# The last two chunks' sums shared with GpSimd, the last chunk's norm on ScalarE, and a new order table

## The chip, the cores and the metric

One core of a Trainium2 chip. The time is the device time of one execution, in microseconds, given as the median of several executions. All the executions quoted count as fast ones in the record. Profiles are of one execution each; its span is about 1.8 us shorter than its time.

## The reference, cut to what matters

```python
x = A_x
x = x + _A_ref(_layernorm(x), ...)   # a state-space layer with complex states
x = x + _B_ref(_layernorm(x), ...)   # a long convolution by FFT, times q (here: the normalised x)
x = x + _A_ref(_layernorm(x), ...)
x = x + _B_ref(_layernorm(x), ...)
return x                             # (1, 2048, 640)
```

The convolution result of B, called Y below, does not depend on x and is made once, in the first part of the kernel. Applying B is then only `x + layernorm(x) * Y`. The kernel works in four chunks of 512 rows, each of four tiles of 128 x 640.

## The kernel before: the parts that matter

Every piece of work is a task with an engine and a priority. A small scheduler runs when the program is built, not on the chip: it simulates the engines with estimated durations and takes the ready task with the lowest number in a table WHEN. The result is one fixed order of instructions for each engine.

```python
WHEN = {"kv_lk0": 0, ..., "a_t0": 26.17, ..., "yt_nsi": 30.27, ..., "yq0_VA:m0": 31.92, ...}   # 862 entries, cut

def run(self):                      # cut
    ...
    when = WHEN[t.name]
    t.rank, t.wait = (-when[0], when[1]) if isinstance(when, tuple) else (-when, 0.3)
    ...
    t = max(cands, key=lambda t: (t.rank, -t.idx))     # among the tasks ready for this engine
    ...
    order.sort(key=lambda t: (t.start, t.idx))         # start as the scheduler's simulation has it
    for t in order:
        t.emit(t.eng)
```

Two tasks that will matter fill tables that are needed much later. Beside them stand the copies out of PSUM, which free the accumulator buffers for TensorE (in the changed kernel TensorE waits 2.77 us for one such copy):

```python
def e_t0(_):                                           # task a_t0, VectorE; read by task a_t1 on ScalarE
    v.tensor_scalar(r, y, MAGIC, None, ALU.add)        # 128 x 1290, f32
    v.scalar_tensor_tensor(r, r, MAGIC, y, ALU.subtract, ALU.subtract)

def e_nsi(_):                                          # task yt_nsi, VectorE: the sign of one table
    nc.vector.tensor_scalar(T["NSi"].get(), T["Si"].get(), -1.0, None, ALU.mult)

def evac(nc, eng, out, in_):                           # a copy out of PSUM
    if eng == "act":
        nc.scalar.activation(out, in_, ACT.Copy)
    else:
        nc.vector.tensor_copy(out, in_)
```

The end of the kernel, B applied to the last chunk tile by tile (the groups have one tile each):

```python
if len(qs) == 1:
    ... nc.vector.scalar_tensor_tensor(b, x, nmean, Y, ALU.add, ALU.mult)     # (x - mean) * Y
    ... nc.vector.scalar_tensor_tensor(Y, b, rstd, x, ALU.mult, ALU.add)      # * rstd + x
else:
    ... ln_apply(...)                                                         # ScalarE or VectorE
    ... nc.vector.tensor_tensor(b, b, Y, ALU.mult)
    ... nc.vector.tensor_tensor(Y, b, x, ALU.add)
```

## Time and profile before

| | before |
|---|---|
| time, median of 3 first runs | 358.5 us (357.69 to 358.55) |
| span of the profiled execution | 356.8 us |
| TensorE busy | 327.5 us, 92% |
| VectorE busy | 315.1 us, 88% |
| ScalarE busy | 256.4 us, 72% |
| last residual sum begins (the last matmul is done) | 345.89 us |

The last row is the best divider of this kernel: what comes before it is ruled by TensorE (327.5 of 345.9 us busy), what comes after it is an 11 us tail of VectorE, ScalarE and one store. The lines themselves stand in the prediction.

### The profile page before, as it was taken

Reading aid. Unit: us, or ns where it says so; the run is one execution under the profiler, and the core shown is the slowest. Engines: PE = TensorE matmul, PEld = TensorE weight load, DVE = VectorE, ACT = ScalarE, POOL = GpSimd, SP = SyncE. Lnnn points to the kernel's source line nnn. Section 1 sums busy time; section 2 is a strip of 40 time slices with the busy share of each in tenths; the row PEclk is TensorE's granted clock in tenths of the full one; section 3 lists DMA queues with packets and bytes.
Section 4 is the critical chain, followed back from the end, with each engine's and each line's share of the span. In section 5 each row is a group of like instructions: output and inputs, shape, how many; then the busy total and the mean of one; then the engine's idle time right before and its main releaser. Section 6 shows DMA issues by size and latency. Waiting matters only on the chain.

```text
span 356.8 us, 8409 instructions
## 1 busy us (share of the span) xinstructions
PE 327.5 (92%) x3534; PEld 247.6 (69%) x3565; DVE 315.1 (88%) x479; ACT 256.4 (72%) x406; POOL 20.8 (6%) x51
## 2 busy tenths in 40 slices
PE   7686998989998997999999999999999999999970
PEld 7346876867686986986685677686866767755640
DVE  8799798798799797999999969979999679999896
ACT  3999798898799999943378599797256577306850
POOL 5841003000000000000000000000000000000000
PEclk9999899999999999999999999999999999999996
DMA  7999999999999982790226690605032022220141
GB/s 193 208 235 188 182 184 217 193 186 202 237 245 163 184 174 46 144 233 2 62 73 119 137 333 34 147 18 132 0 68 81 3 16 59 75 75 2 50 172 73
DMA packets 118712, 45.91 MB, mean 129 GB/s; under 512 B 111629, under 2 KB 112914, under 8 KB 118674
## 3 DMA queue, kind: packets, MB, share of 16 engines
q1 hardware_dynamic: 118528, 45.36, 59.9%
q8 instruction: 28, 0.46, 0.5%
q14 instruction: 10, 0.08, 0.1%
q10 hardware_dynamic: 146, 0.01, 0.0%
HBM read 17.38 MB, written 7.86 MB: 71 GB/s over the span
## 4 chain that ended last, share of the span: by engine, by line
PE 69%; ACT 10%; DVE 8%; DMA 7%; issue 3%; SPq 2%; DVEq 0%; ACTq 0%
PE ps L859 31%; PE ps L770 11%; PE ps L773 11%; ACT b L382 6%; PE ps L608 3%; PE ps L1163 3%; DMA b<-in_A_C_im_dram 2%; DMA b<-in_B_v_dram 2%; DVE b L1169 2%; PE ps L1313 2%; DMA b<-b 2%; PE ps L1314 1%; PE ps L1208 1%; SPq L536 1%; DMA b<-in_B_k_dram 1%
## 5 line engine op out<-in xcount | busy, mean ns | idle before, releaser
L382 ACT ACTIVATE b<-ps 128x1024 bf16<-128x1024 f32 (+3 forms) x125 | 109.6, 945 | 29.5 <-PE ps L773 25.5
L859 PEld LDWEIGHTS <-b 128*128 128x128 bf16 x880 | 67.7, 98 | 48.3
L859 PE MATMUL ps<-W,b 128*128 128x128 bf16 (+1 forms) x629 | 95.7, 298 | 0.6
L770 PE MATMUL ps<-b,BT 128*128 128x256 bf16 x400 | 56.8, 273 | 0.0
L773 PE MATMUL ps<-b,BT 128*128 128x256 bf16 x400 | 56.7, 273 | 0.0
L808 DVE TENSOR_TENSOR_SCAN b<-rtab,b 128x1290 bf16<-128x1290 f32 x16 | 44.7, 2833 | 0.3
L773 PEld LDWEIGHTS <-BT 128*128 128x128 bf16 x400 | 39.1, 98 | 4.5
L770 PEld LDWEIGHTS <-BT 128*128 128x128 bf16 x400 | 38.6, 98 | 4.4
L726 ACT ACTIVATE b<-b,nmr,rstd 128x640 bf16<-128x640 f32 (+1 forms) x43 | 37.0, 915 | 6.2 <-DVE nmr L693 6.2
L681 ACT ACTIVATE junk<-b,nmean 128x640 bf16<-128x640 f32 x48 | 39.7, 828 | 1.5
L1232 PE MATMUL ps<-b,b 128*128 128x128 bf16 x170 | 35.1, 219 | 1.2 <-ACT G L382 0.7
L1235 PE MATMUL ps<-b,b 128*128 128x128 bf16 x170 | 35.4, 219 | 0.0
L1237 PE MATMUL ps<-b,b 128*128 128x128 bf16 x150 | 32.8, 219 | 0.0
L1234 PE MATMUL ps<-b,b 128*128 128x128 bf16 x150 | 32.8, 219 | 0.0
L384 DVE CAST b<-ps 128x1024 bf16<-128x1024 f32 (+2 forms) x24 | 26.2, 1109 | 6.3 <-PE ps L1208 2.7
L867 ACT ACTIVATE b<-ps 128x640 f32<-128x640 f32 x16 | 11.1, 697 | 22.8 <-PE ps L859 22.8
L859 PE MATMUL ps<-G,b 128*128 128x128 bf16 (+1 forms) x152 | 26.5, 295 | 0.4
L1163 PE MATMUL ps<-b,fd 128*128 128x512 bf16 x73 | 18.6, 380 | 3.8 <-POOL fd L1141 2.0
L1313 PE MATMUL ps<-b,b 128*128 128x128 bf16 x160 | 19.4, 219 | 2.6 <-ACT b L382 2.1
L1314 PE MATMUL ps<-b,b 128*128 128x128 bf16 x160 | 19.2, 219 | 0.0
L552 ACT ACTIVATE b<-b,s_F 128x640 f32<-128x640 bf16 x20 | 17.2, 859 | 1.8 <-DVE W L556 1.4
L556 DVE SCALAR_TENSOR_TENSOR W<-b,s_F 128x640 bf16<-128x640 bf16 x20 | 17.4, 882 | 1.0 <-ACT b L552 0.7
(210 smaller groups left out, 560.3 us busy)
## 6 DMA issues: line engine op xcount, KB each, us to landing
b<-in_A_x_dram SPq DMA_DIRECT2D x8, 640.0 KB, 4.9
b<-ysd SPq DMA_DIRECT2D x8, 640.0 KB, 5.1
b<-in_B_ssm_k_dram SPq DMA_DIRECT2D x5, 512.0 KB, 8.6
kvd<-b SPq DMA_DIRECT2D x5, 512.0 KB, 4.3
b<-kvd SPq DMA_DIRECT2D x5, 512.0 KB, 5.4
ysd<-b SPq DMA_DIRECT2D x5, 512.0 KB, 5.0
out_dram<-b SPq DMA_DIRECT2D x8, 320.0 KB, 2.2
tab<-in_A_B_re_dram SPq DMA_DIRECT2D x1, 800.0 KB, 7.4
```

The lines of the kernel that those rows point to most:

```text
L382: nc.scalar.activation(out, in_, ACT.Copy)
L681: nc.scalar.activation(small.junk, src(q), ACT.Square, bias=st["nmean"][:, i:i + 1], scale=1.0, accum_out=st["ssq"][:, i:i + 1])
L726: nc.scalar.activation(dst, src, ACT.Identity, bias=st["nmr"][:, i:i + 1], scale=st["rstd"][:, i:i + 1])
L770: nc.tensor.matmul(pb[:, jj, c2, :], lhsT=aw["BT1"][:, c2, j, k, :], rhs=uT[:, 0:2, k, :], start=(k == 0), stop=False)
L773: nc.tensor.matmul(pb[:, jj, c2, :], lhsT=aw["BT0"][:, c2, k, j * P:(j + 1) * P], rhs=uT[:, 2:4, k, :], start=False, stop=(k == NJ - 1))
L808: nc.vector.tensor_tensor_scan(gv, rt, gv, 0.0, ALU.mult, ALU.add)
L859: nc.tensor.matmul(pc[:, o0:o1], lhsT=lh, rhs=rh, start=(n == 0), stop=(n == len(ops) - 1))
L1163: nc.tensor.matmul(pk[:, 512 * b:512 * (b + 1)], lhsT=s_ds.get()[:, l, :], rhs=kT[:, t0:t0 + 512], start=(l == 0), stop=(l == 3))
L1232: nc.tensor.matmul(ps[:, g, 0, :], lhsT=T["Cf"].get()[:, q, :], rhs=are, start=True, stop=single)
L1234: nc.tensor.matmul(ps[:, g, 0, :], lhsT=T["Sf"].get()[:, q, :], rhs=A[:, 2 * q + 1, :], start=False, stop=True)
L1235: nc.tensor.matmul(ps[:, g, 1, :], lhsT=T["NSf"].get()[:, q, :], rhs=are, start=True, stop=single)
L1237: nc.tensor.matmul(ps[:, g, 1, :], lhsT=T["Cf"].get()[:, q, :], rhs=A[:, 2 * q + 1, :], start=False, stop=True)
```

## The change

Its intent: VectorE is the second busiest engine and alone in the tail. Of the four last tiles, three get their norm from ScalarE, sums may go to GpSimd, which is idle there (20.8 us busy in the whole span, nothing after 60 us), and each tile is stored when it is done. As this changes the tasks, the order table was searched anew.

```diff
 WHEN = {
-    (862 entries)
+    (867 entries: nearly every number is another)
 }
@@ b_chunk
-        if out is not None and q % 2 == 1:
+        if out is None:
+            return
+        if len(groups) > 1:
+            ... one store for each tile of 128 rows
+        elif q % 2 == 1:
             ... one store for two tiles
@@
-            if len(qs) == 1:
+            if qs[0] == 3:
                 ... the pair of two-input instructions
@@
-                        else:
-                            nc.vector.tensor_tensor(s_Y.get()[:, q, :], b, x, ALU.add)
-                    t_m = S.add(f"{nm}_m:{q}", "dve", 0.83 if out is None else 0.77, [t_mm], ...)
+                        else:
+                            (nc.gpsimd if eng == "pool" else nc.vector).tensor_tensor(s_Y.get()[:, q, :], b, x, ALU.add)
+                    engs, ests = (("dve", "pool"), (0.77, 1.4)) if out is not None and c >= NCH - 2 else ("dve", 0.83 if out is None else 0.77)
+                    t_m = S.add(f"{nm}_m:{q}", engs, ests, [t_mm], ...)
```

## The prediction

The sum for the tail came to -0.6 us: -1.8 us for the norm on ScalarE and -0.1 us for the single stores, and about +1.3 us for the lock. "The lock" is the name for the longer times of GpSimd's and VectorE's instructions beside each other; the trace shows them around 25 us (2.67 us below), but not how long they would be in the tail, so the +1.3 us were not shown. Without the lock the sum was -1.9 us. The 0.41 us for the multiply are 0.49 us less 0.08 us of overlap (the pair's instructions of 0.88 us step by 0.80). The 0.49 us can be had from the trace before, as an estimate: the products all in bf16 take 1.29 us for 128x2176 and 1.49 us for 128x2560, and a line through the two gives 0.49 us at 128x640.

> **What bounds the kernel now.** I read the page first (busy shares, then the 40 slices), then busy time by stretches of the span, then the last pieces of the chain of waits and the timeline of the end. Every reading below is of the one profiled execution, 356.8 us long (358.5 us is the median of the timed runs).
>
> ```profile
> PE 327.5 (92%) x3534; PEld 247.6 (69%) x3565; DVE 315.1 (88%) x479; ACT 256.4 (72%) x406; POOL 20.8 (6%) x51
> ...
> POOL 5841003000000000000000000000000000000000
> ```
>
> TensorE is the busiest engine, VectorE is close behind, and GpSimd does nothing after its first setup work. Where is TensorE's missing 8%? The stretches say (columns: busy us and instruction count of PE, PEld, DVE, ACT, POOL, then granted clock, DMA share, GB/s):
>
> ```profile
> 0.00:36.00 36.00, 26.33 (x323) 20.65 (x325) 30.84 (x99) 29.40 (x45) 17.83 (x45) 1.00 0.99 208
> 36.00:72.00 36.00, 33.83 (x511) 27.71 (x509) 29.32 (x30) 32.18 (x39) 2.94 (x6) 0.95 1.05 192
> 72.00:108.00 36.00, 34.47 (x462) 26.16 (x466) 30.96 (x50) 31.37 (x42) 0.00 (x0) 1.00 1.12 216
> 108.00:144.00 36.00, 32.27 (x478) 28.45 (x477) 30.68 (x50) 35.52 (x44) 0.00 (x0) 1.00 0.79 137
> 144.00:180.00 36.00, 35.90 (x371) 28.27 (x372) 34.86 (x32) 18.91 (x27) 0.00 (x0) 1.00 0.52 111
> 180.00:345.80 165.80, 164.75 (x1404) 116.39 (x1419) 150.71 (x211) 107.60 (x208) 0.00 (x0) 1.00 0.31 82
> 345.80:356.80 11.00, 0.00 (x0) 0.00 (x0) 7.69 (x13) 1.42 (x4) 0.00 (x0) 0.73 0.30 119
> ```
>
> Three regimes. The head, 0 to 144 us, leaves TensorE idle 9.7 + 2.2 + 1.5 + 3.7 = 17.1 us. From 144 to 345.8 us it is idle 1.2 us: this is its own work and no reordering shortens it. The tail, 11.0 us after the last matmul, is all idle. So the time is head idle plus TensorE work plus tail; the change can gain only in the head (by the new order table) and in the tail.
>
> The tail, from the timeline:
>
> ```profile
> 345.89 0.81 DVE L871 SCALAR_TENSOR_TENSOR b<-ps,b 128x640 f32<-128x640 f32 x1
> 346.63 0.88 DVE L901 SCALAR_TENSOR_TENSOR b<-b,nmean,b 128x640 bf16<-128x640 f32 x1
> 347.55 0.89 DVE L905 SCALAR_TENSOR_TENSOR b<-b,rstd,b 128x640 bf16<-128x640 bf16 x1
> 348.35 2.47 DVE L901 SCALAR_TENSOR_TENSOR b<-b,nmean,b 128x640 bf16<-128x640 f32 x3
> 350.86 1.68 DVE L905 SCALAR_TENSOR_TENSOR b<-b,rstd,b 128x640 bf16<-128x640 bf16 x2
> 352.45 0.16 DVE L691 RECIPROCAL rstd<-std 128x1 f32<-128x1 f32 x1
> 352.72 0.88 DVE L905 SCALAR_TENSOR_TENSOR b<-b,rstd,b 128x640 bf16<-128x640 bf16 x1
> 353.63 0.33 SPq L887 DMA_DIRECT2D out_dram<-b  x1
> ```
>
> After the last residual sum (L871) VectorE alone works: eight two-input instructions for the four tiles of the last chunk, each starting 0.80 us after the one before, ending at 353.60, then one store; 3.2 us later the program ends. ScalarE is done at 348.2 us.
>
> [...] This trace's GpSimd tensor_tensor of 128x128 takes a median 394 ns[...]. [...]
>
> ```profile
> 25.12 0.33 DVE L481 TENSOR_SCALAR s_lam<-s_lam 128x5 f32<-128x5 f32 x1
> 25.48 2.31 DVE L487 TENSOR_TENSOR b<-ident_bf,s_lam 128x1920 bf16<-128x1920 bf16 x1
> ...
> 25.38 2.67 POOL L1141 TENSOR_TENSOR fd<-ident_bf,skf 128x128 bf16<-128x128 bf16 x2
> ```
>
> Two GpSimd instructions that take 0.39 us each elsewhere take 2.67 us around a 2.31 us VectorE one; and 128x5 instructions beside GpSimd take 0.33 to 0.37 us against 0.16 us. [...] 128x2560 all bf16 takes 1.49 us, yet the sum with a float32 input 0.82 us for a quarter of that.
>
> **The change part by part.** Every engine's instruction order of the changed kernel was read beside the old one. TensorE has 7123 rows in both: no work is added to it.
>
> *Last chunk, norm by ScalarE.* For three of four tiles the pair "add mean, times Y" and "times rstd, plus x" (2 x 0.80 us) becomes a ScalarE normalisation (0.91 us, as L726 in this profile), a bf16 multiply and a sum. [...] the sum steps by 0.74 us (three in 2.29 us). The fourth tile keeps the old pair. Old tail after the last residual sum: 346.63 to 353.60, 6.97 us. New order there on VectorE: multiply, multiply, sum, pair's first half, reciprocal and product, pair's second half, multiply, sum: 0.41 x 2 + 0.74 + 0.80 + 0.27 + 0.80 + 0.41 + 0.82 = 4.66 us, plus about 0.5 us of hand-overs (0.1 us each at dependent steps, as between 347.43 and 347.55): 5.2 us. ScalarE's statistics of the last tile end at 348.23 in the old timing, before VectorE's reciprocal would come (349.1), and its normalisation, 0.91 us, lies beside the pair's second half, 0.80 us. So the tail is 1.8 us shorter, if nothing contends.
>
> *Sums on GpSimd.* Only three move: two of the last but one chunk and one of the last. They take three times 0.74 us off VectorE[...]. [...]
>
> *Single stores.* 160 KB instead of 320 KB last; issue 0.33 us and 2.2 us to landing are mostly not size: -0.1 us, an estimate.
>
> [...]
>
> *The new order table.* It moves nearly every instruction of the head: the small multiplications that feed GpSimd's first tables now stand 7th in TensorE's order instead of second, the other half of the B matrix is loaded first. The 17.1 us of head idle can grow or shrink; the numbers in the table are priorities, and I take no time from them. Nothing in the profile gives a sign. I put 0 with a spread of about 2 us.
>
> Predicted: 358.5 - 0.6 = 357.9, rounded down a little because a tuned kernel is seldom given a new table that was seen to lose: 357.5 us.
>
> **The rivals.** First, no lock at the tail: GpSimd's sums hide and the tail gives its full 1.9 us, 356.6 us. [...] Against it: the 2.67 us above. Second, the lock in full plus a late last residual sum: 358.5 us or slightly more, the change pays nothing; for it speaks that VectorE is busy without a gap from 345.89 on[...]. Third, the head decides: TensorE waits for a transfer or a table that now comes later, 360 us or 355 us; for it speaks that the DMA share is about 1.0 in the first 108 us[...], and that the first 36 us alone hold 9.7 us of idle.
>
> **Range and chances.** Tail -1.9 to +0.4, head -2.5 to +2.5 in eight of ten: 355.0 to 360.5 us. Two per cent is 7.2 us, more than the whole gain open to the tail and over 40% of the head's idle: faster 0.02, slower 0.03, same 0.95.
>
> **What would show it.** In the changed profile: from the last residual sum's end to VectorE's last end, 5.2 us means no lock[...]. The last ScalarE normalisation must lie beside the pair's second half. TensorE's idle up to 144 us, 17.1 us before, gives the table's part; if it moves by over 3 us the head decided and the tail's story is secondary. The stretch from 144 us to the last matmul must hold about 1 us of idle again; if it holds several, the new order starved TensorE late and my division of the time is wrong.

## The result

The changed kernel takes 363.04 us (median of 4 runs, 362.35 to 363.43), the kernel before 358.38 us in the same rounds. The ratio is 1.0132, 95% interval 1.0111 to 1.0153. All ratios here are the mean time of one kernel's fast runs over that of the other's of the same rounds, so they are not quite the ratio of the medians quoted. Within 2% that is "the same"; in fact the kernel is slower, clear of the noise, and the time lies outside the predicted range.

**Where it went.** The last residual sum begins at 351.43 us instead of 345.89: 5.54 us are lost before it. After it the tail is 361.4 - 351.43 = 10.0 us instead of 10.9: about 1 us is won there. So the tail did what it was meant to do and the rest of the program was made slower. The same stretches of the span as in the prediction, for the changed kernel (the same columns; the last stretch begins just before the last residual sum):

```profile
0.00:36.00 36.00, 29.62 (x327) 22.57 (x327) 31.31 (x98) 27.10 (x44) 17.86 (x45) 0.91 0.97 198
36.00:72.00 36.00, 32.15 (x446) 25.81 (x445) 28.63 (x29) 27.91 (x36) 2.25 (x6) 0.91 0.96 175
72.00:108.00 36.00, 32.97 (x465) 24.88 (x460) 27.55 (x33) 30.79 (x38) 0.00 (x0) 1.00 1.05 217
108.00:144.00 36.00, 33.09 (x482) 28.79 (x480) 32.15 (x64) 35.85 (x48) 0.00 (x0) 1.00 0.81 157
...
351.30:361.40 10.10, 0.10 (x2) 0.00 (x0) 6.69 (x11) 3.24 (x6) 1.59 (x1) 0.72 0.27 97
```

Here lies a trap. TensorE's idle time up to 144 us is 6.4 + 3.9 + 3.0 + 2.9 = 16.2 us, less than the 17.1 us before, and still the head lost over 5 us. Idle time of a fixed stretch says little when the amount of work done in it differs. Look at the counts instead: weight loads up to 144 us (one belongs to each matmul, and no record of them is missing: both traces hold 3565) were 325 + 509 + 466 + 477 = 1777 before and are 327 + 445 + 460 + 480 = 1712 now. All but one of the 65 missing ones are in the second stretch, 445 instead of 509, and there the granted clock is 0.91. At a lower clock TensorE counts as busy for longer with the same work: a matmul of 128x128 takes 0.31 us in this stretch at half clock and 0.22 us before it.

**What happens around 36 us.** VectorE and TensorE of the changed kernel, from the timeline (start, duration, engine, line, operation; in square brackets the idle time before and what ended it):

```profile
35.02 0.83 DVE L639 TENSOR_SCALAR b<-rtab 128x1290 f32<-128x1290 f32 x1
35.88 1.50 DVE L640 SCALAR_TENSOR_TENSOR b<-b,rtab 128x1290 f32<-128x1290 f32 x1
37.30 0.72 DVE L1000 TENSOR_SCALAR b<-b 128x2176 bf16<-128x2176 bf16 x1
37.94 2.35 DVE L385 CAST b<-ps 128x1024 bf16<-128x1024 f32 x2
...
```

```profile
39.21 0.61 PE L1217 MATMUL ps<-FA,b 64*128 64x128 bf16 x8 [2.77 <-DVE b L385]
```

The first two lines are the task a_t0, the third is yt_nsi. They take 37.94 - 35.02 = 2.92 us, and only then come two copies out of PSUM (CAST). TensorE waits 2.77 us for the first of them. From within this wait on, from 38.2 to 45.0 us by the trace's clock record, TensorE has half its clock. The kernel before has the same tasks, but elsewhere:

```profile
28.85 0.82 DVE L638 TENSOR_SCALAR b<-rtab 128x1290 f32<-128x1290 f32 x1
...
34.25 0.72 DVE L991 TENSOR_SCALAR b<-b 128x2176 bf16<-128x2176 bf16 x1
34.88 0.82 DVE L384 CAST BT<-ps 128x640 bf16<-128x640 f32 x1
```

There a_t0 holds nobody up, and only the 0.72 us of yt_nsi stand before a copy that TensorE waits for (1.7 us). Both tables mean a_t0 to come earlier than it does: the old one puts it at 26.17 us and it ran at 28.85, 2.7 us late; the new one puts it at 28.86 and it ran at 35.02, 6.2 us late. (The table holds priorities, but here they can be read as times: the scheduler's own simulation, run again from the two kernels, starts this task at 25.97 and at 28.77 us.) The new table puts the first copy behind it, for tile yq0_VA, at 31.78 us; it ran at 37.94. So in the new order VectorE reaches this place about 6 us behind its plan; the order is fixed, and the urgent copy, behind 2.92 us of the two tasks, came at 37.94 us.

**The tail.** VectorE from the last residual sum on, and GpSimd's sum:

```profile
351.43 0.82 DVE L872 SCALAR_TENSOR_TENSOR b<-ps,b 128x640 f32<-128x640 f32 x1 [0.18 <-PE ps L860]
...
352.18 0.89 DVE L924 TENSOR_TENSOR b<-b,b 128x640 bf16<-128x640 bf16 x2
353.11 1.91 DVE L932 TENSOR_TENSOR b<-b,b 128x640 bf16<-128x640 bf16 x1
...
357.60 0.82 DVE L932 TENSOR_TENSOR b<-b,b 128x640 bf16<-128x640 bf16 x1
```

```profile
347.23 4.01 POOL L932 TENSOR_TENSOR b<-b,b 128x640 bf16<-128x640 bf16 x2 [282.39 <-DVE b L924]
352.75 1.59 POOL L932 TENSOR_TENSOR b<-b,b 128x640 bf16<-128x640 bf16 x1 [1.51 <-DVE b L924]
```

One sum takes VectorE 0.82 us at the end and 1.91 us beside GpSimd's. The residual sum itself waited only 0.18 us, for TensorE: GpSimd did not delay it. From the end of the residual sum (352.18) to VectorE's end (358.42) it is 6.2 us, against 7.0 before.

### The profile page after: what moved, and what is told of

Read it like the earlier page. It is cut to its first block, busy times and chain, and to the rows that moved or that the text cites. A ratio compares the mean times of both kernels' runs of the same rounds, so it can differ in the third digit from the quotient of the medians.

```text
span 361.4 us, 8447 instructions
## 1 busy us (share of the span) xinstructions
PE 334.2 (92%) x3565; PEld 250.6 (69%) x3565; DVE 315.6 (87%) x477; ACT 257.2 (71%) x408; POOL 25.7 (7%) x54
## 4 chain that ended last, share of the span: by engine, by line
PE 57%; ACT 5%; DMA 2%; DVE 1%; issue 1%; ACTq 0%
PE ps L860 33%; PE ps L771 10%; PE ps L774 10%; ACT b L383 2%; DMA b<-b 2%; PE ps L1322 1%; PE ps L1323 1%; DVE b L932 1%; ACT rtab L649 0%; ACT tab L647 0%; PE ps L1241 0%; ACT L645 0%; ACT tab L645 0%; PE ps L1217 0%; ACT rtab L646 0%
## 5 line engine op out<-in xcount | busy, mean ns | idle before, releaser
L383 ACT ACTIVATE b<-ps 128x1024 bf16<-128x1024 f32 (+2 forms) x123 | 106.0, 923 | 36.6 <-PE ps L774 26.2
L1241 PE MATMUL ps<-b,b 128*128 128x128 bf16 x170 | 35.6, 222 | 3.2 <-ACT b L383 2.7
L385 DVE CAST b<-ps 128x1024 bf16<-128x1024 f32 (+1 forms) x26 | 30.3, 1188 | 8.2 <-PE ps L1246 5.2
L1244 PE MATMUL ps<-b,b 128*128 128x128 bf16 x170 | 35.9, 222 | 0.0
L1243 PE MATMUL ps<-b,b 128*128 128x128 bf16 x150 | 33.4, 223 | 0.0
L1246 PE MATMUL ps<-b,b 128*128 128x128 bf16 x150 | 33.4, 222 | 0.0
L860 PE MATMUL ps<-G,b 128*128 128x512 bf16 (+1 forms) x160 | 27.0, 299 | 0.0
L932 POOL TENSOR_TENSOR b<-b,b 128x640 bf16<-128x640 bf16 x3 | 5.6, 1877 | 283.9 <-DVE b L924 283.9
L1172 PE MATMUL ps<-b,fd 128*128 128x512 bf16 x80 | 20.3, 405 | 1.1 <-DVE b L385 0.8
L1322 PE MATMUL ps<-b,b 128*128 128x128 bf16 x160 | 19.2, 219 | 1.7 <-DVE b L1178 1.6
L1217 PE MATMUL ps<-FA,b 64*128 64x128 bf16 x320 | 15.3, 228 | 5.1 <-DVE b L385 2.8
L1323 PE MATMUL ps<-b,b 128*128 128x128 bf16 x160 | 19.1, 219 | 0.0
```

The lines of the kernel that those rows point to most:

```text
L860: nc.tensor.matmul(pc[:, o0:o1], lhsT=lh, rhs=rh, start=(n == 0), stop=(n == len(ops) - 1))
L1241: nc.tensor.matmul(ps[:, g, 0, :], lhsT=T["Cf"].get()[:, q, :], rhs=are, start=True, stop=single)
L1243: nc.tensor.matmul(ps[:, g, 0, :], lhsT=T["Sf"].get()[:, q, :], rhs=A[:, 2 * q + 1, :], start=False, stop=True)
L1244: nc.tensor.matmul(ps[:, g, 1, :], lhsT=T["NSf"].get()[:, q, :], rhs=are, start=True, stop=single)
L1246: nc.tensor.matmul(ps[:, g, 1, :], lhsT=T["Cf"].get()[:, q, :], rhs=A[:, 2 * q + 1, :], start=False, stop=True)
```

## The experiments

Twelve kernels ran, in three groups of four; each is compared with runs of the kernel before on the same chip (medians 358.02, 358.03 and 357.86 us; the third group has the eleven runs of the second and one more). To compare two kernels of different groups, compare their ratios.

### 1 and 2: the table and the tail taken apart

The tasks of the second use of B on its last three chunks and of the last copies of the layer before it make up the tail; all others are the head. In the first kernel the code of the change stays, with the old table's numbers for the head; in the second the old code gets the new table's numbers for the head.

```diff
 # old_table_new_tail: the changed kernel
-WHEN = new table
+WHEN = old table, but the new table's entries for the tail and for the new tasks
 # new_table_old_tail: the kernel before
-WHEN = old table
+WHEN = new table, but the old table's entries for the tail
```

> The changed kernel's code with the old order table for everything but the end (the last chunk's and the two chunks' final multiplications and sums keep the new entries). TensorE's order is that of the kernel before but for the last two groups, which change places. If the loss of 5.5 us up to the last matmul comes from the new table's order of the head, this kernel has its last matmul at 345.8 us as before and the changed tail of 10.0 us: 357.4 us, 1.0 us faster than before. If the loss comes from the code of the tail (GpSimd, stores) in some hidden way, it is near 363 us.

Measured: 356.62 us, ratio 0.9962 (0.9946 to 0.9979). The last residual sum begins at 345.93 us, as before.

> The reverse: the code of before, with the new order table for everything but the end. If the head's order is the cause: last matmul at 351.4 us and the old tail of 11.0 us, 364.0 us. If the tail's code is the cause: 358.4 us.

Measured: 363.12 us, ratio 1.0143 (1.0125 to 1.0161). So the new table costs 1.4% by itself, and the new tail by itself gains 0.4%, some 1.4 us. The prediction's two parts have opposite signs, and the table is the larger one. The split is not perfectly clean: in the second run's trace the last residual sum begins at 349.63 us, only 3.7 us later than before, and what follows it takes 11.7 us instead of 10.9.

### 3: without GpSimd

```diff
-engs, ests = (("dve", "pool"), (0.77, 1.4)) if out is not None and c >= NCH - 2 else ("dve", ...)
+engs, ests = ("dve", ...)
```

> The changed kernel with its three shared sums back on VectorE, nothing else changed. If GpSimd's sums and VectorE's two-input instructions hold each other up[...]: the 1.91 us sum and the 0.81 us small product in the end of VectorE's chain fall back to 0.82 and 0.16 us, and two sums of 0.74 us come back to VectorE before the last residual sum, where there is little room; the tail after the last matmul goes from 10.0 to about 8.7 us, 361.7 us. If GpSimd's help is real, the kernel gets slower, 364 us or more.

Measured: 363.57 us, ratio 1.0138 (1.011 to 1.0167): no gain, a miss. VectorE got three sums of 0.74 us back, 2.2 us in all, and the fixed order put one of them and a normalisation behind the last residual sum. That about cancels what the sum beside GpSimd's had cost (1.91 us instead of 0.82). The run changes two things at once and settles nothing about that; experiments 8 and 12 are the better test.

### 4: the half clock filled up

Idle matmuls into an unused corner of buffers that TensorE owns at that moment, in the two places where it waits; no wait and no order is changed (the table is shortened here).

```diff
+FILL = {'a_b01:1': 10, 'yq0_KA:m0': 8, 'a_p1': 12, 'yq0_VA:m3': 40}      # matmuls after this task, 128 x 128
+nc.tensor.matmul(slot.get()[:, 896:1024], lhsT=ident, rhs=ident, start=True, stop=True)
```

> The changed kernel with 70 idle matmuls of 128x128 put into TensorE's two waits of the head (30 between 12.6 and 17 us, 40 in the wait from 36.4 to 39.2 us), into unread columns of PSUM; no other engine's order or waits change. Clock theory: the two stretches at half the clock (6.8 us each in the changed kernel, one of 3.4 us in the kernel before) follow from too little work in these waits; filled, they vanish, mean clock rises from 0.972 to 0.99 or more, and the time falls by up to the 6.8 us that the half clock costs, 356.5 to 359 us. Wait theory: the half clock only falls into time that TensorE would have waited through anyhow, or the order's waits are the loss: the clock may rise but the time stays within 1 us of 363.0.

Measured: 362.11 us, ratio 1.0107 (1.0082 to 1.0132); the interval overlaps that of the changed kernel. The granted clock rose from 0.970 to 0.973 there to between 0.981 and 0.990. The slices show it, first the changed kernel, then the profiled execution of this one, its fastest (tenths of full clock in 40 slices of 9 us):

```profile
PEclk9789699999999999999999999999999999999996
```

```profile
PEclk9999999999999999999999999999999999999995
```

In the median only 0.9 us come back. But the clock is fully repaired in only two executions of six: those at 0.990 took 360.2 and 361.2 us, the four at 0.981 to 0.985 took 361.5 to 362.9. One stretch of 3.4 us at half clock lowers the mean of a span of 360 us by 0.005, so these four still had one or two of them (an estimate). The kernel before shows the same dependence: its six executions of this group at 0.978 to 0.980 took 358.6 us on average, its five at 0.982 to 0.987 took 357.7.

TensorE's order of tasks is the same in both kernels, so in the profiled execution one can ask when the same piece of work begins. The changed kernel's 400th weight load begins at 45.23 us; here, idle ones not counted, at 41.24. The lead was 1.4 us just before the wait and 1.6 us just after it, so the wait is about as long as before; the rest, 2.4 us, was won where the changed kernel has half its clock. At the 1900th load the lead is still 4.4 us (153.24 against 157.60); then TensorE waits 2.5 us for a transfer, 1.0 us in the changed kernel:

```profile
160.83 0.72 PE L777 MATMUL ps<-b,BT 128*128 128x256 bf16 x5 [2.51 <-DMA b<-b]
```

2.9 us are left at the end. So where the half clock goes altogether, 1.9 and 2.9 us of the loss of 4.7 us come back, more than the wait theory allows and less than the clock theory expected. The half clock is a part of the loss and no mere companion; how large a part in the other executions is not shown, as they have no profile.

### 5 and 6: which section of the table

A task is early if either table puts it before 45 us; 179 are.

```diff
 # old_start
+WHEN[k] = old[k] if k is early else new[k]
 # new_start
+WHEN[k] = new[k] if k is early or in the tail else old[k]
```

> The changed kernel; the 179 tasks that either table puts before 45 us take the old priorities, all others the new ones. Counted against the same amount of TensorE work, the changed kernel is 3.5 us behind the kernel before by then and another 2.2 us from there to the end. Theory A (the new order loses in several places, each for itself): old table with new tail 356.6 + 2.2 = 358.8 us. Theory B (all of it is lost in the first 45 us): 356.6 us. Theory C (all of it is lost later): 362 us or more.

Measured: 369.19 us, ratio 1.0317 (1.0278 to 1.0355). None of the theories expected this. The waits of TensorE between 118 and 138 us say where it comes from (us in total, times, longest):

```profile
PE ps L1250 <- DVE b L394: 4.3, 2, 4.1
PE ps L1250 <- ACT b L392: 3.0, 2, 2.7
```

Up to there this kernel is ahead of the changed one; then two new waits of 4.1 and 2.7 us come. In the changed kernel TensorE has a task of 4.6 us (A1c0_bp:1) before this place; with the joined table the scheduler puts it behind. For the longer wait, TensorE needs a copy that stands behind 4.1 us of statistics on VectorE (121.92 to 126.02 us): the same kind of wait as at 36 us. So these are waits that neither kernel has, made by joining the tables. As a test of the theories the run is spoilt.

> The complement: the tasks before 45 us take the new priorities, the rest the old ones, with the new tail. Theory A: 356.6 + 3.5 = 360.1 us. Theory B: 362 us or more. Theory C: 357 us.

Measured: 361.42 us, ratio 1.0100 (1.0073 to 1.0126). With the early section alone most of the loss is there. The time lies between theories A and B, and since joining tables makes waits of its own, as the run beside it shows, it is a hint and no proof.

### 7: the tasks before the two copies, moved behind them

This leaves the table alone and moves two tasks in the finished order.

```diff
         order.sort(key=lambda t: (t.start, t.idx))
+        late = [t for t in order if t.name in ("a_t0", "yt_nsi")]
+        order = [t for t in order if t not in late]
+        at = [t.name for t in order].index("yq0_VA:e3") + 1
+        order[at:at] = late
```

> The changed kernel with two of VectorE's tasks (the table fill of 0.83 + 1.50 us and the sign change of 0.72 us) moved behind the two copies out of PSUM, for which TensorE waits 2.77 us at 36.45 us. If this wait is a loss by itself and nothing takes its place: 363.0 - 2.3 = 360.7 us or a little less, if the half clock after it goes too. If another wait takes its place at once, 363.0 us.

Measured: 362.22 us, ratio 1.0111 (1.0084 to 1.0138), only 0.8 us less than the changed kernel. VectorE and TensorE show why:

```profile
37.67 0.82 DVE L643 TENSOR_SCALAR b<-rtab 128x1290 f32<-128x1290 f32 x1
...
40.58 0.22 DVE L1272 TENSOR_TENSOR b<-b,kd 128x16 bf16<-128x16 bf16 x1
```

```profile
40.86 0.39 PE L1221 MATMUL ps<-FA,b 64*128 64x128 bf16 x6 [2.66 <-DVE b L1272]
```

The wait has not gone, it has moved. Behind the copies stands a tiny product of 0.22 us (task yq1_ka) that TensorE needs next; the two tasks now stand before that one, and TensorE waits 2.66 us there. A verdict on the theory at this point would have been wrong: the same 3 us of work that nobody needed yet still stood before something urgent.

### 8: a GpSimd that does not read

On the first experiment's kernel. The result is wrong: the sum of one tile is replaced by zeros.

```diff
-(nc.gpsimd if eng == "pool" else nc.vector).tensor_tensor(s_Y.get()[:, q, :], b, x, ALU.add)
+if eng == "pool" and len(groups) > 1:
+    nc.gpsimd.memset(s_Y.get()[:, q, :], 0.0)
+else: ... as before
```

> Old table and new tail, with GpSimd's sum in the last chunk put as a memset, which writes the same tile but reads none (a wrong result on purpose). If GpSimd's reads hold VectorE up, VectorE's sum beside it takes 0.82 us instead of 1.91 and the time is 356.6 - 1.1 = 355.5 us; if the longer sum has another cause, it stays at 1.9 us and the time at 356.6 us.

Measured: 355.57 us, ratio 0.9931 (0.9906 to 0.9955). VectorE's sum beside GpSimd, and GpSimd's instruction, first with the sum (old table, new tail), then with the memset:

```profile
347.60 1.91 DVE L940 TENSOR_TENSOR b<-b,b 128x640 bf16<-128x640 bf16 x1
```

```profile
347.30 1.52 POOL L940 TENSOR_TENSOR b<-b,b 128x640 bf16<-128x640 bf16 x1 [1.57 <-issue]
```

```profile
346.73 0.83 DVE L943 TENSOR_TENSOR b<-b,b 128x640 bf16<-128x640 bf16 x1
```

```profile
346.40 0.63 POOL L941 MEMSET b<- 128x640 bf16 x1 [1.54 <-issue]
```

Both pairs overlap in time, the second for 0.3 us only, as the memset is also shorter; of the two, only the sum beside the reading instruction takes VectorE 1.91 us. It ends at 349.51, when GpSimd's sum has ended (348.82) and the sum's own step of 0.74 us has passed. VectorE's part of the tail is 6.2 us (346.68 to 352.90) with the sum and 5.2 us (345.80 to 350.96) with the memset. So the sum beside GpSimd's reading instruction costs VectorE 1.1 us here.

### 9, 10 and 11: moved behind all three, and further

```diff
 # three_moved: as two_moved, with
+        at = [t.name for t in order].index("yq1_ka") + 1
 # five_moved: in addition
+        ("a_wm04:0", "a_wm03:1") behind "kv_ev4:0"
 # five_moved_filled: five_moved with the idle matmuls of experiment 4
```

> As two_moved, but the two tasks stand one place later, also behind the 0.22 us product for which TensorE then waited 2.66 us; VectorE is idle there afterwards, for 2.5 to 4.1 us. The table fill is not needed before 112 us. If the wait at 36.45 us is a loss by itself, it is now gone: 363.0 - 2.7 = 360.3 us or less. If again another wait takes its place: 362 to 363 us.

Measured: 358.60 us, ratio 1.0020 (0.9990 to 1.0050). Moving two tasks by three places in one engine's order gives 4.4 us back by the medians, 4.0 us by the ratios (1.0132 against 1.0020). That is more than the 2.8 us of the wait; the half clock after it went as well. VectorE, and the second of the four stretches of before:

```profile
35.10 2.57 DVE L390 CAST b<-ps 128x1024 bf16<-128x1024 f32 x2
37.59 0.22 DVE L1273 TENSOR_TENSOR b<-b,kd 128x16 bf16<-128x16 bf16 x1
37.67 0.82 DVE L644 TENSOR_SCALAR b<-rtab 128x1290 f32<-128x1290 f32 x1
```

```profile
36.00:72.00 36.00, 32.58 (x505) 26.33 (x507) 33.27 (x34) 32.03 (x41) 2.25 (x6) 1.00 1.08 193
```

The copies come at 35.10 instead of 37.94 us, the longest wait of TensorE between 34 and 45 us is 0.5 us, the clock in this stretch is 1.00 again, and 507 weight loads are done in it: 509 before, 445 in the changed kernel. The half clock from 14.4 to 21.2 us stays, and the time is good in spite of it.

The same can be seen at equal work, computed from the traces by a script. Taking from the traces how long each of TensorE's 220 tasks lasts up to the start of the next, and subtracting the shortest such duration that any of twelve kernels shows, one has how far each kernel is behind the work alone (us). The levels depend on what is counted as a task's start; the differences between columns do so by a few tenths.

| TensorE work done | before | changed | three_moved | old table, new tail |
|---|---|---|---|---|
| 25 us | 11.2 | 11.2 | 11.0 | 12.2 |
| 30 us | 13.3 | 16.7 | 11.5 | 12.7 |
| 90 us | 20.6 | 25.8 | 21.1 | 20.0 |
| 145 us | 26.4 | 32.0 | 27.6 | 26.5 |

After 30 us of work the changed kernel is 5.2 us behind its own version with two tasks moved, after 25 us only 0.2 us, and 4.4 us of that are still there at the end of the head. Of these 5.2 us, 2.8 are the wait; the rest falls together with the half clock after it, and is about what was won there in the profile of experiment 4 (2.4 us). The half clock went in both ways, by filling the wait and by removing it, so in these profiles it goes with the wait and not with the table as such.

> As three_moved, and the two weight products (1.67 us) that stand before the product on which TensorE waits 1.11 us at 86 us are put behind it. If the losses add up: 1.1 us less than three_moved, some 359.2 us. If the later order takes it back: as three_moved.

Measured: 357.77 us, ratio 0.9998 (0.9974 to 1.0022). The interval overlaps that of three_moved, so a gain is not shown. TensorE's waits from 70 to 100 us:

```profile
PE ps L1246 <- ACT b L388: 1.4, 1, 1.4
PE ps L1222 <- ACT b L388: 1.3, 1, 1.3
PE ps L1327 <- DVE b L1183: 1.0, 1, 1.0
```

The wait that was to go (the last line) is still 1.0 us long: now the product itself comes late, as VectorE stands idle for 2.97 us before it, waiting for a transfer (of in_B_v). Two waits for ScalarE stand beside it, 1.4 and 1.3 us; before the one of 1.3 us, ScalarE had waited 1.83 us for one of the weight products that were moved back. Losses of such an order do not simply add up.

> five_moved with the 70 idle multiplications of filled_gaps. Theory: the new table loses by waits in its order and by the half clock that these waits bring on; with both taken away the time comes within 1 us of old table with new tail, 356.6 to 357.6 us. If something else in the new table costs time (transfers, ScalarE), it stays at 359 us or more.

Measured: 360.84 us, ratio 1.0078 (1.0049 to 1.0107), 3.1 us slower than without the fill. A miss for the theory. The trace does not show the idle matmuls in the way where they stand: the 1900th weight load, idle ones not counted, begins at 152.77 us, against 154.43 in five_moved. Then TensorE waits 2.7 us for a transfer, 0.6 us in five_moved, and 3.4 us of half clock follow:

```profile
160.53 1.25 PE L782 MATMUL ps<-b,BT 128*128 128x256 bf16 x5 [2.68 <-DMA b<-b]
```

By the 2000th load it is 2.0 us behind. Nor was all of the half clock taken away: 3.4 us of it stay at 13.6 us. Why the transfer comes late in both kernels with idle matmuls was not followed.

### 12: the last chunk's sum back on VectorE

On the first experiment's kernel; the two sums of the chunk before stay on GpSimd.

```diff
-... if out is not None and c >= NCH - 2 else ...
+... if out is not None and c == NCH - 2 else ...
```

> Old table and new tail, the last chunk's one sum back on VectorE (the two of the chunk before stay on GpSimd). VectorE does one sum of 0.74 us more, its other sum takes 0.82 us instead of 1.91, and the reciprocal then finds its input ready: 356.6 - 0.35 to -0.7 = 355.9 to 356.3 us. If the help outweighs the lock: 357 us or more.

Measured: 356.01 us, ratio 0.9955 (0.9931 to 0.9979). VectorE's part of the tail is 5.7 us (346.47 to 352.19) instead of 6.2, as expected. In the whole time this does not stand out from the 0.9962 of the first experiment. It is, with that one, the best correct version: 0.4% faster than the kernel before and 1.7% faster than the changed one.

## Why the prediction was wrong

**The step that failed** is "The new order table": "Nothing in the profile gives a sign. I put 0 with a spread of about 2 us." It measured +5.5 us in the traces up to the last residual sum and +1.4% in the runs (new_table_old_tail), 5.1 us. What the runs show in its place: two tasks of VectorE, 2.9 us long, stand before two copies out of PSUM and one small product for which TensorE waits 2.8 us, and TensorE's clock is halved for 6.8 us from within this wait on; putting the two tasks behind takes 4.0 us of the loss away (4.4 by the medians). The remaining part, 2 us by three_moved against old_table_new_tail (1.0020 against 0.9962), is lost between 30 and 90 us of TensorE's work, by the table above; which waits it is stays open.

**There was a sign.** The order of VectorE's instructions, which was read before predicting, shows the table fill, read much later by a ScalarE task that the table places at 116.09 us, ahead of the copies. And the profile before showed both that such a copy is waited for (1.7 us at 34 us, behind yt_nsi) and that VectorE was 2.7 us behind its table already. I compared the orders for what was moved and did not ask of each move: who waits for the instruction behind it?

**The third rival**, that the head decides and the time is 360 us, was nearest in direction and wrong in its cause: TensorE did not wait for a transfer or a table that came later, but for VectorE, which did something else first. The chance of "same" was right only because 2% is 7 us.

**TensorE's own work.** "The time is head idle plus TensorE work plus tail" took the work as a fixed time, and that failed too: TensorE's busy time rose from 327.5 to 334.2 us with the same 3565 weight loads (31 matmul records missing in the trace before are some of it, the half clock is more: 13.7 us of it in the head against 3.4). The 7123 rows that the prediction counts stand in no record; the two traces have 3565 weight loads each. From 144 us on TensorE is idle for 1.05 us in the changed kernel as well (34.95 busy of 36.00 and 171.30 of 171.30); that step holds. The check named for the head, idle time up to 144 us, fails: it fell by 0.9 us while the head lost over 5.

**The tail, predicted -0.6 us.** About 1 us was won in the trace, 1.4 us in the runs; the direction was right, the size too small. Term by term:

- Norm by ScalarE, without the lock: VectorE's part was put at 5.2 us and is 5.2 us with the memset. The multiply was put at 0.49 us and takes 0.49. ScalarE's last normalisation does lie beside the pair's second half, and VectorE waited only 0.2 us for it.
- The lock: VectorE's sum beside GpSimd's takes 1.91 us instead of 0.82, 1.1 us more, and VectorE's part of the tail is 6.2 us instead of the 5.2 with the memset. GpSimd's sum starts 0.3 to 0.4 us before VectorE's.
- A late last residual sum: nothing. A small 128x1 product ahead of it took 0.81 us instead of 0.16 and ended, at 351.25 us, within 0.02 us of the end of GpSimd's other two sums, but there VectorE had time to spare.
- GpSimd's sum: 1.52 and 1.59 us in the last chunk. The two of the chunk before took 4.01 us together, beside VectorE's two-input instructions; whether these lengthened them no run tests alone.
- Single stores, -0.1 us: from VectorE's end to the end of the span 3.0 us instead of 3.2; a store of 160 KB lands in 1.8 us, one of 320 KB in 2.2 (medians).

## What to carry to other kernels

VectorE, 6 us behind its plan in a fixed order, did 2.92 us of work that nobody needed yet before two copies, for the first of which TensorE waited 2.77 us. So work that nobody needs soon must stand behind the copies that free another engine's buffers, however early the plan says it will be done. Read a new order by asking, for each long instruction, who waits for the next ones, and compare two traces at equal work done, not over equal stretches of time. A wait can also cost more than its length: here 2.8 us of it came with 6.8 us of half clock, and some 4 us went when both went. A wait of 2.66 us (two_moved) came with 3.4 us of half clock, and one of 1.69 us in the kernel before was followed by 3.4 us of it. When a wait only moves after an edit, move the cause past everything that is urgent before giving up the theory.
